# Attention feeding a gated feed-forward layer: two state reads moved from chunk 0 to chunks 3 to 5, and one intermediate kept on chip

## The chip, the cores and the metric

The kernel runs on one core of one Trainium2 chip. A core has five engines with a queue of instructions each: PE (TensorE, the matmul array), DVE (VectorE), ACT (ScalarE), POOL (GpSimd) and SP (SyncE, which here only starts transfers). The metric is the time of one execution on the device in microseconds (us); a run of the same kernel differs from another by about 0.3%.

## The reference

A batch has 8 heads, 512 tokens and 32 state rows of 64 numbers. Tokens attend to the state rows ("xread"), state rows attend to the tokens ("sread"); both go, as 4608 rows of 512, through a feed-forward layer with 2048 hidden units. `x` is scaled up by 3.377, the two weights are given in 64 bits.

```python
B, H, S, Ns, D = 8, 8, 512, 32, 64          # d_model = H * D = 512, d_ff = 2048
scores  = scale * matmul(x, state.T)        # (B, H, S, Ns)
a       = exp(scores - max);  a  /= a.sum(-1) + 1e-9
xread   = matmul(a, state)
scores2 = scale * matmul(state, x.T)        # the same numbers, transposed
a2      = exp(scores2 - max); a2 /= a2.sum(-1) + 1e-9
sread   = matmul(a2, x)
x = concatenate([xread, sread], axis=2).transpose(0, 2, 1, 3).reshape(B * (S + Ns), H * D)
h = x @ w_in
return (h - tanh(h)) @ w_out
```

## The kernel before

**Chunks and steps.** The 512 tokens of batch i are chunk i (0 to 7); the 256 state rows of all batches are chunk 8. A chunk has 16 steps, one for each 128 hidden units, and step `st = 16*i + f` of the outer loop writes the hidden units two steps ahead (`LAG = 2`, `hidden`), whatever is planned for that step, and then the output matmuls of its own step (`output`). So batch 0's last part is written in steps 0 to 15, batch 4's in steps 64 to 79.

**The feed-forward layer.** xread is never formed. Since `(a @ state) @ w_in = a @ (state @ w_in)`, `hidden` multiplies the attention weights `aT` with `m = state @ w_in` of that batch into the bank `hps` (L375, L376, L377: each 32-bit factor is split into a rounded part and a rest, and three of the four products are kept). `finish` takes tanh on ACT and subtracts on DVE (both L383: tile `t`), then `split` makes `g`: the rounded part on ACT (L90), the rest on DVE (L91). `add` accumulates into `ops` from `g` and the converted `wo`: rounded `g` by rounded `wo` (L413), rounded `g` by the rest of `wo` (L414), the rest of `g` by rounded `wo` (L415). The rest of `wo` comes from DVE, its rounded part from ACT.

**Chunk 0 carries the conversions.** The weights come in as 64-bit numbers and are made into 32-bit ones, block by block (16 blocks `wo0` to `wo15` of `w_out`, 16 blocks `wqp` of `w_in`): DVE L120, DVE L121, ACT L123, DVE L124. A block of `w_out` is then split into `wo` (ACT L90, DVE L91). A block of `w_in` goes to DRAM (`wf`) and is at once multiplied by the states of batches 0 and 1 (`m_first_two`, L149). Batch 0's half of the result is copied by ACT to `m_first` (L150). Batch 1's half is copied to a tile `stage` (L152), written to DRAM (L153, for the first four blocks L587 and L590), and read back in chunk 0 and 1 as `mr` (L200). The same products for batches 2 to 7 are made later by `m_units` (`wst`, L186, L187, L188, L191), with two buffers of `stage`.

**Attention of a batch** (`attention`): scores by matmul into `sps`, copied to `s` (L273), then the softmax over states on a transposed copy `e`, transposed back to `at` and split into `aT`. Batches 0 and 1 (`b < LONE`) use block-diagonal states and 64 columns of the array (L254, and L517 for batch 0), the others 32 columns in eight tiles (L262). **The state read** (`state_read`) starts from the same scores `s`: for each half of the heads DVE takes a maximum (L306) and makes small factors (L308, L312, L313), ACT the exponential in place (L310), SP loads the tokens `xn` (L316, 512 KB), PE turns the weights (`pps`, L319), ACT copies them (`p2t`, L321), PE multiplies (`rps`, L329: 64 columns for `b < LONE`, else 32), and DVE scales the result into `sr` (L335, four instructions). `sr` is read in chunk 8 only. In batch 0 the state read also splits `at` into `aT0`, with the rest made on POOL.

**What sets the order.** The start is written out by hand (`SEQ`). After it, a table (`SCH`) says in which step each part of `conv`, `wo`, `pair` (the calls of `m_first_two`), `a0` (batch 0's state read, four parts), `att` (the attention of batches 1 to 7, with their state reads) and `m0`, `m1` (the units) is written; a scheduler then orders each engine's instructions from that, and `tc.issue_after(x)` holds an instruction behind `x`. All transfers stand in SP's queue in one order.

Of the kernel before, what the change touches and what calls it, by code (L numbers as in the profile page):

```python
# [9 lines left out]
F32 = mybir.dt.float32  # L10
# [9 lines left out]
P = 128  # L20
B, H, S, NS, D = 8, 8, 512, 32, 64
# [6 lines left out]
LAG = 2  # L28
LONE = 2


@with_exitstack
def attention_ffn(ctx: ExitStack, tc: tile.TileContext, xT, xn, bd, bh, sp, sm, sl, win, wout, xout, sout):
# [106 lines left out]
    XSUB = nc.gpsimd if '1' else None  # L140

    def m_first_two(q, p):
# [6 lines left out]
        nc.tensor.matmul(ps, sps[:, p], wfs[q, k][:, c], start=True, stop=True)  # L149
        nc.scalar.copy(m_first[q][64 * c : 64 * c + 64, k], ps[0:64])  # L150
        stage = pool.tile([P, 2, 512], F32, tag="stage", name=f"st0{q}{p}", bufs=SB)
        nc.scalar.copy(stage[64:128, 0], ps[64:128])  # L152
        nc.sync.dma_start(  # L153
            mdram[1][q][0][k, 2 * c : 2 * c + 2].rearrange("h n f -> (h n) f"), stage[64:128, 0]
        )

# [37 lines left out]
    def load_m(b, q):  # L194
        if b == 0:
            r = m_first[q]
# [36 lines left out]
    def attention(b, aT):  # L233
# [51 lines left out]
        for hf in range(2):  # L285
# [224 lines left out]
    def step(op):  # L510
# [7 lines left out]
        elif k == "c":  # L518
            ss[j] = pool.tile([P, 512], F32, tag="s", name=f"s0{j}")
            o(nc.scalar.copy(ss[j], sps_ps[j]))  # L520
# [60 lines left out]
        elif k == "R":  # L581

            if j % 2 == 0:
                stages[j // 2] = pool.tile([P, 4, 256], F32, tag="stage", name=f"st00{j}", bufs=SB)
            st = stages[j // 2]
            with tc.issue_after(tanhs[RE[j]][0]):
                nc.scalar.copy(st[64:128, :, P * (j % 2) : P * (j % 2) + P], mps[j][64:128])  # L587
            if j % 2:
                for k in range(2):
                    nc.sync.dma_start(  # L590
                        mdram[1][0][0][k, :, :, P * (j - 1) : P * (j + 1)].rearrange("(c h) n f -> (h n) c f", c=2),
                        st[64:128, 2 * k : 2 * k + 2],
                    )

# [50 lines left out]
    for i in range(B + 1):  # L645
        for f in range(NFF):
# [24 lines left out]
            for b in range(1, B):  # L671
                n = D0["att"][str(b)].count(st)
                if n:
                    if b not in atts:
                        atts[b] = new_attention(b)
                    advance(atts[b], n)
            for g in range(2):
                advance(m1[g], D0[f"m{g}"].count(st))
            chunks[i].output(f)
# [49 lines left out]
```

## Time and profile before

| | |
|---|---|
| median of 3 runs | 688.42 us (687.70 to 689.92) |
| the profiled execution | 688.88 us, of which the profile's span is 687.1 us |
| granted TensorE clock, mean over the span | 0.988 |
| busy share of the span | PE 96%, DVE 67%, ACT 55%, POOL 1% |
| moved by DMA | 99.30 MB, 145 GB/s on average |

Chunk 0's output matmuls end near 142 us. In the profile an instruction's row gives its start, its duration, its engine, its line in the kernel and the tiles that it writes and reads. Of matmuls in a row the starts are the measure: they overlap by about 0.17 us. A number in brackets behind a row is the time that the engine was idle before it, and what it waited for. "PEld" loads the weights of a matmul beside PE. The clock column gives the share of full speed that the PE's clock was granted.

### The profile page before, as it was taken

What the parts mean: (1) busy time and instruction counts of PE and PEld (TensorE: products, weight loads), DVE (VectorE), ACT (ScalarE), POOL (GpSimd) and SP (SyncE); (2) the same over time, 40 slices, a digit from 0 to 9 for tenths busy, and PEclk for the clock granted to TensorE, in tenths of its full rate; (3) what the DMA queues carried; (4) which work ended last, traced back from release to release, by engine and by line L of the source; (5) the groups of instructions that cost most, each with busy time, mean ns of one, the idle gap of its engine ahead of it and who ended that gap; (6) DMA issues with size and microseconds to landing.
All of it is one profiled execution on the core that took longest, in us unless ns stands there. A gap on an engine that the chain in (4) does not pass through costs nothing.

```text
span 687.1 us, 9286 instructions
## 1 busy us (share of the span) xinstructions
PE 660.5 (96%) x3386; PEld 521.7 (76%) x3386; DVE 458.2 (67%) x803; ACT 377.9 (55%) x663; POOL 6.6 (1%) x11
## 2 busy tenths in 40 slices
PE   4788988999999999999999999999999999999997
PEld 2446666888788887888788878887878788888896
DVE  5897999965695559556876568546853587434442
ACT  3768876766675655457656555634433354333342
POOL 2100000000000000000000000000000000000000
PEclk9899998999999999999999999999999999999999
DMA  8888972555545552345536432643241312001310
GB/s 292 252 300 257 340 275 93 183 185 144 169 122 188 150 168 97 124 126 162 175 124 203 133 106 86 220 145 127 89 157 44 124 48 95 28 14 41 131 32 31
DMA packets 46317, 99.30 MB, mean 145 GB/s; under 512 B 6208, under 2 KB 12096, under 8 KB 46272
## 3 DMA queue, kind: packets, MB, share of 16 engines
q1 hardware_dynamic: 46272, 98.72, 44.4%
q8 instruction: 26, 0.43, 0.3%
q14 instruction: 19, 0.16, 0.1%
HBM read 66.72 MB, written 31.98 MB: 144 GB/s over the span
## 4 chain that ended last, share of the span: by engine, by line
PE 85%; DMA 6%; DVE 4%; ACT 3%; issue 1%; SPq 0%; ACTq 0%; DVEq 0%
PE ops L413 17%; PE ops L414 17%; PE ops L415 17%; PE hps L376 9%; PE hps L377 9%; PE hps L375 9%; PE mps L187 2%; PE sps L262 1%; PE rps L329 1%; DMA mr<-md 1%; PE mps L186 1%; DMA w01d<-in_win 1%; DMA wf<-w 1%; PE pps L319 1%; DMA w31d<-in_win 1%; DMA wo1d<-in_wout 1%
## 5 line engine op out<-in xcount | busy, mean ns | idle before, releaser
L414 PE MATMUL ops<-wo,g 128*128 128x512 f32 x544 | 215.5, 396 | 2.1 <-DVE wo L91 2.1
L413 PE MATMUL ops<-wo,g 128*128 128x512 f32 x544 | 208.1, 397 | 3.1 <-ACT wo L90 3.1
L415 PE MATMUL ops<-wo,g 128*128 128x512 f32 x544 | 208.4, 394 | 0.0
L383 DVE TENSOR_TENSOR t<-hps,t 128x512 f32<-128x512 f32 (+1 forms) x142 | 93.3, 658 | 98.4 <-ACT t L383 97.5
L383 ACT ACTIVATE t<-hps 128x512 f32<-128x512 f32 (+1 forms) x142 | 81.1, 573 | 133.7 <-PE hps L377 131.4
L413 PEld LDWEIGHTS ops<-wo,g 128*128 128x128 f32 x544 | 102.4, 189 | 32.1 <-ACT wo L90 5.8
L90 ACT CAST g<-t 128x512 fp32r<-128x512 f32 (+1 forms) x142 | 84.6, 596 | 72.9 <-DVE t L383 56.6
L414 PEld LDWEIGHTS ops<-wo,g 128*128 128x128 f32 x544 | 103.2, 190 | 26.5 <-DVE wo L91 3.3
L91 DVE TENSOR_TENSOR g<-t,g 128x512 fp32r<-128x512 f32 (+1 forms) x142 | 93.3, 657 | 42.4 <-ACT g L90 41.1
L415 PEld LDWEIGHTS ops<-wo,g 128*128 128x128 f32 x544 | 102.8, 189 | 24.5 <-issue 2.4
L375 PE MATMUL hps<-aT,m 128*128 128x512 f32 x248 | 98.3, 397 | 0.0
L377 PE MATMUL hps<-aT,m 128*128 128x512 f32 x248 | 97.1, 393 | 0.6 <-DVE m L91 0.6
L376 PE MATMUL hps<-aT,m 128*128 128x512 f32 x248 | 97.0, 391 | 0.0
L377 PEld LDWEIGHTS hps<-aT,m 128*128 128x128 f32 x248 | 46.7, 188 | 11.0 <-DVE m L91 1.0
L91 DVE TENSOR_TENSOR wst<-w,wst 64x512 fp32r<-64x512 f32 x64 | 43.9, 686 | 16.4 <-ACT wst L90 15.0
L375 PEld LDWEIGHTS hps<-aT,m 128*128 128x128 f32 x248 | 46.6, 188 | 10.5 <-issue 0.7
L376 PEld LDWEIGHTS hps<-aT,m 128*128 128x128 f32 x248 | 46.7, 188 | 10.0 <-issue 0.5
L91 DVE TENSOR_TENSOR m<-mr,m 128x1024 fp32r<-128x1024 f32 x31 | 37.8, 1220 | 9.3 <-ACT m L90 8.6
L188 ACT COPY st<-mps 128x512 f32<-128x512 f32 x64 | 36.7, 587 | 12.3 <-PE mps L187 12.0
L90 ACT CAST wst<-w 64x512 fp32r<-64x512 f32 x64 | 39.6, 619 | 1.8 <-ACT wo13r L123 1.0
L90 ACT CAST m<-mr 128x1024 fp32r<-128x1024 f32 x31 | 32.3, 1043 | 7.3 <-DMA mr<-md 7.2
L187 PE MATMUL mps<-wst,sms 128*128 128x512 f32 x64 | 24.7, 394 | 0.0
(218 smaller groups left out, 587.6 us busy)
## 6 DMA issues: line engine op xcount, KB each, us to landing
md<-st SPq DMA_DIRECT2D x144, 128.0 KB, 2.2
mr<-md SPq DMA_DIRECT2D x28, 512.0 KB, 4.0
xT<-in_xT SPq DMA_DIRECT2D x16, 512.0 KB, 4.6
xn<-in_xn SPq DMA_DIRECT2D x16, 512.0 KB, 4.2
w<-wf SPq DMA_DIRECT2D x16, 512.0 KB, 4.6
out_x<-ob SPq DMA_DIRECT2D x32, 256.0 KB, 2.1
wn<-wf SPq DMA_DIRECT2D x8, 512.0 KB, 3.8
ml<-md SPq DMA_DIRECT2D x8, 512.0 KB, 3.6
```

The costliest lines, as they stand in the source:

```text
L90: nc.scalar.copy(hi, src)
L91: return (sub or nc.vector).tensor_sub(lo, src, hi)
L186: nc.tensor.matmul(ps, s[:, 1, h], t[:, e], start=True, stop=False)
L187: nc.tensor.matmul(ps, s[:, 0, h], t[:, e], start=(g == 1), stop=True)
L188: nc.scalar.copy(stage[:, e], ps)
L375: nc.tensor.matmul(ps, mhi[k][:, cols], ahi[:, k], start=(k == 0), stop=False)
L376: nc.tensor.matmul(ps, mhi[k][:, cols], alo[:, k], start=False, stop=False)
L377: nc.tensor.matmul(ps, mlo[k][:, cols], ahi[:, k], start=False, stop=(k == nk - 1))
L383: tanhs.append((nc.scalar.activation(t, ps, AF.Tanh).ins, nc.vector.tensor_sub(t, ps, t).ins))
L413: nc.tensor.matmul(o, g[:, 0, tok], wo[:, f, 0], start=(f == 0), stop=False)
L414: nc.tensor.matmul(o, g[:, 0, tok], wo[:, f, 1], start=False, stop=False)
L415: return nc.tensor.matmul(o, g[:, 1, tok], wo[:, f, 0], start=False, stop=(f == NFF - 1)).ins
```

## The change

- **State reads.** The state reads of batches 0 and 1 leave `attention`. Batch 0's four parts (`a0`) go from steps 0, 0, 1, 13 to 58, 60, 62, 64, batch 1's (`r1`, before at the end of its attention in steps 11 and 13) to 74, 76, 78, 80. Their scores `s` stay in four tiles of their own until then (`EARLY_S = 2`). The split of `aT0`, which stood in batch 0's state read, is written in the start, and its rest is made on DVE instead of POOL.
- **Batch 1's state @ w_in stays on chip.** `m_second[q]` takes the place of `stage` and DRAM: 16 writes of 128 KB and 4 reads of 512 KB go. For q = 0 and 1 it sits in the two `stage` buffers. The four copies of the first four blocks (L587) become eight of half the size.
- **Columns.** `LONE = 1`: batch 1's scores use the eight tiles of 32 columns, and the state reads of batches 0 and 1 the 32-column form.
- **Order.** In steps below 48 (`GATED`) what is planned for a step is held behind the tanh pair of that step, and the first four `m0` units go from steps 11, 11, 15, 15 to 16, 17, 18, 19.

```diff
-LONE = 2
+GATED = 48
+EARLY_S = 2
+LONE = 1
...
+    def second(q):
+        if q < 2:
+            return pool.tile([P, 2, 512], F32, tag="stage", name=f"mr1{q}", bufs=SB)
+        return pool.tile([P, 2, 512], F32, tag=f"mr1{q}", name=f"mr1{q}", bufs=1)
...
+            m_second[q] = second(q)
         ps = bank(ps_a, f"mps0{q}{p}")
         nc.tensor.matmul(ps, sps[:, p], wfs[q, k][:, c], start=True, stop=True)
         nc.scalar.copy(m_first[q][64 * c : 64 * c + 64, k], ps[0:64])
-        stage = pool.tile([P, 2, 512], F32, tag="stage", name=f"st0{q}{p}", bufs=SB)
-        nc.scalar.copy(stage[64:128, 0], ps[64:128])
-        nc.sync.dma_start(
-            mdram[1][q][0][k, 2 * c : 2 * c + 2].rearrange("h n f -> (h n) f"), stage[64:128, 0]
-        )
+        nc.scalar.copy(m_second[q][64 * c : 64 * c + 64, k], ps[64:128])
...
-        yield from state_read(b, ss)
+        if b >= EARLY_S:
+            yield from state_read(b, ss)
+        else:
+            late[b] = ss
...
+    def late_read(b):
+        yield from state_read(b, late[b])
+
+    def split_first():
+        for hf in range(2):
+            split(aTs[0][:, 0, hf], aTs[0][:, 1, hf], ats[hf])
...
-                split(aTs[0][:, 0, hf], aTs[0][:, 1, hf], ats[hf], nc.gpsimd if P0[4] else None)
...
-            w = 2 if b < LONE else 1
+            w = 1
...
     a0 = state_read(0, ss)
+    split_first()
+    late1 = late_read(1)
...
-    SCH = ... "a0": [0, 0, 1, 13], ... "m0": [11, 11, 15, 15, 20, ...
+    SCH = ... "a0": [58, 60, 62, 64], ... "m0": [16, 17, 18, 19, 20, ... "r1": [74, 76, 78, 80]
...
-            with tc.issue_after(first):
+            with ExitStack() as gates:
+                if st < GATED:
+                    for x in tanhs[st]:
+                        gates.enter_context(tc.issue_after(x))
                 advance(a0, D0["a0"].count(st))
+                advance(late1, D0["r1"].count(st))
                 ... attention and units, now inside the same block
```

The lines of the changed file stand a little lower: L90, L91 become L94, L95; L120, L121, L124 become L124, L125, L128; L149 becomes L161; L310, L319, L329 become L327, L336, L346; L383 becomes L400; L413, L414, L415 become L430, L431, L432.

**PE, early in chunk 0** (`pps00` and `rps00` are the first half of batch 0's state read, `pps01` begins the second; `mps013` is the product of `w_in` block 13 with the two states; `ops0_0` is the output bank of chunk 0, tokens 0 to 127). Before:

```order
L319 MATMUL pps00_369<-ident_72,s00_150 128x128 x4
L329 MATMUL rps00_376<-xn00_367,p2t00_374 64x128 x8
L149 MATMUL mps013_432<-w011_321,sps_126 128x512
L413 MATMUL ops0_0_389<-wo_77,g0_2_345 128x512
L413 MATMUL ops0_1_390<-wo_77,g0_2_345 128x512
L413 MATMUL ops0_2_391<-wo_77,g0_2_345 128x512
L413 MATMUL ops0_3_392<-wo_77,g0_2_345 128x512
L319 MATMUL pps01_449<-ident_72,s01_161 128x128 x4
L149 MATMUL mps020_562<-w020_468,sps_126 128x512
```

After:

```order
L161 MATMUL mps012_340<-w011_313,sps_118 128x512
L161 MATMUL mps013_387<-w011_313,sps_118 128x512
L430 MATMUL ops0_0_344<-wo_77,g0_2_337 128x512
L430 MATMUL ops0_1_345<-wo_77,g0_2_337 128x512
L430 MATMUL ops0_2_346<-wo_77,g0_2_337 128x512
L430 MATMUL ops0_3_347<-wo_77,g0_2_337 128x512
L161 MATMUL mps020_498<-w020_403,sps_118 128x512
```

The two parts of the state read no longer stand between the products `mps012`, `mps013`, `mps020` and the output matmuls of step 2. The first half's read now stands at row 1253 of PE's 2780, near the end of chunk 3.

**SP, the same time** (`xn` are the tokens of a state read, `md100` batch 1's product in DRAM, `wo1d` the raw second block of `w_out`). Before:

```order
L316 DMA xn00_367<-in_xn 128x1024
L552 DMA wf0_120<-w000_164 512x1x128
L316 DMA xn01_447<-in_xn 128x1024
L109 DMA w11d_198<-in_win 128x1024
L552 DMA wf0_120<-w000_164 512x1x128
L109 DMA w12d_236<-in_win 128x1024
L552 DMA wf0_120<-w002_217 512x1x128
L109 DMA w13d_256<-in_win 128x1024
L590 DMA md100_84<-st000_272 64x2x256 x2
L109 DMA wo1d_290<-in_wout 128x1024
L552 DMA wf0_120<-w002_217 512x1x128
```

After:

```order
L113 DMA w10d_174<-in_win 128x1024
L569 DMA wf0_112<-w000_156 512x1x128
L113 DMA w11d_190<-in_win 128x1024
L569 DMA wf0_112<-w000_156 512x1x128
L113 DMA w12d_228<-in_win 128x1024
L569 DMA wf0_112<-w002_209 512x1x128
L113 DMA w13d_248<-in_win 128x1024
L113 DMA wo1d_285<-in_wout 128x1024
```

The load of `wo1d` had two loads of `xn` and two writes of `md100` ahead of it, and has none of them now. Further down, the twelve writes of L153 leave their places between the loads of the weights, and both loads of `xT1` stand ahead of `wo5d`, where one of them stood behind `wo10d`.

**DVE, at the end of the conversions** (`wor14` and `wor15` are the last blocks of `w_out`; `wo_77<-` is the rest of a block, for which L414 waits). Before:

```order
L121 SCALAR_TENSOR_TENSOR wor15_1092<-wo15d_863,wor15_1092 128x512
L91 TENSOR_TENSOR wst003_1239<-w1001_1219,wst003_1239 64x512 x2
L91 TENSOR_TENSOR wo_77<-wor14_970,wo_77 128x512
L335 TENSOR_SCALAR sr0_78<-rps01_1138,ri01_444 32x64 x4
L91 TENSOR_TENSOR g1_0_1191<-t1_0_1188,g1_0_1191 128x512
L124 ISA wor15_1092<-wor15_1092,wo15r_1093 128x1024
L335 TENSOR_SCALAR sr0_78<-rps11_1151,ri11_1025 32x64 x4
L383 TENSOR_TENSOR t1_2_1288<-hps1_2_1281,t1_2_1288 128x512
L91 TENSOR_TENSOR wo_77<-wor15_1092,wo_77 128x512
```

After:

```order
L125 SCALAR_TENSOR_TENSOR wor14_864<-wo14d_778,wor14_864 128x512
L125 SCALAR_TENSOR_TENSOR wor15_925<-wo15d_788,wor15_925 128x512
L95 TENSOR_TENSOR g0_15_968<-t0_15_965,g0_15_968 128x512
L128 ISA wor14_864<-wor14_864,wo14r_865 128x1024
L128 ISA wor15_925<-wor15_925,wo15r_926 128x1024
L95 TENSOR_TENSOR g1_0_996<-t1_0_993,g1_0_996 128x512
L400 TENSOR_TENSOR t1_2_1055<-hps1_2_1048,t1_2_1055 128x512
L95 TENSOR_TENSOR wst002_1163<-w1001_1161,wst002_1163 64x512 x2
L95 TENSOR_TENSOR wo_77<-wor14_864,wo_77 128x512
L95 TENSOR_TENSOR m12_1344<-mr12_497,m12_1344 128x1024
L95 TENSOR_TENSOR wo_77<-wor15_925,wo_77 128x512
```

The eight scalings `sr` are gone from between the last two rests of `wo`; the rest of `wor14` and of `wor15` stand closer together, and the split of `m12` stands between them.

More of the change, by code (lines that the diff above doesn't have):

```diff
@@ L72, in attention_ffn @@
         [[dram.tile([2, 4, NS, 512], F32, name=f"md{b}{q}{i}") for i in range(1 if b < 6 else 2)] for q in range(NQ)]
+        if b >= 2
+        else None
         for b in range(B)
@@ L140, in attention_ffn @@
     XSUB = nc.gpsimd if '1' else None
+    m_second = {}
+    def second(q):
+        if q < 2:
+            return pool.tile([P, 2, 512], F32, tag="stage", name=f"mr1{q}", bufs=SB)
+        return pool.tile([P, 2, 512], F32, tag=f"mr1{q}", name=f"mr1{q}", bufs=1)
     def m_first_two(q, p):
@@ L194, in load_m @@
     def load_m(b, q):
-        if b == 0:
-            r = m_first[q]
+        if b < 2:
+            r = (m_first, m_second)[b][q]
         else:
@@ L271, in attention @@
             ps = pss[hf]
-            s = pool.tile([P, 512], F32, tag="s", name=f"s{b}{hf}")
+            s = pool.tile([P, 512], F32, tag=f"s{b}{hf}" if b < EARLY_S else "s", name=f"s{b}{hf}", bufs=1 if b < EARLY_S else 2)
             nc.scalar.copy(s, ps)
@@ L295, in attention @@
             yield split(aT[:, 0, hf], aT[:, 1, hf], at)
-        yield from state_read(b, ss)
+        if b >= EARLY_S:
+            yield from state_read(b, ss)
+        else:
+            late[b] = ss
+    late = {}
+    def late_read(b):
[3 more added lines that the diff above has]
+            split(aTs[0][:, 0, hf], aTs[0][:, 1, hf], ats[hf])
     def state_read(b, ss):
-        if b == 0:
-            for hf in range(2):
-                split(aTs[0][:, 0, hf], aTs[0][:, 1, hf], ats[hf], nc.gpsimd if P0[4] else None)
         for hf in range(2):
@@ L498, in attention_ffn @@
     m_first[0] = pool.tile([P, 2, 512], F32, tag="mr", name="mr00", bufs=RRB)
-    wb, stages, mps, sps_ps, hps, ss = {}, {}, {}, {}, {}, {}
+    wb, mps, sps_ps, hps, ss = {}, {}, {}, {}, {}
     es, ms, zs = {}, {}, {}
@@ L518, in step @@
         elif k == "c":
-            ss[j] = pool.tile([P, 512], F32, tag="s", name=f"s0{j}")
+            ss[j] = pool.tile([P, 512], F32, tag=f"s0{j}", name=f"s0{j}", bufs=1)
             o(nc.scalar.copy(ss[j], sps_ps[j]))
@@ L581, in step @@
         elif k == "R":
-            if j % 2 == 0:
-                stages[j // 2] = pool.tile([P, 4, 256], F32, tag="stage", name=f"st00{j}", bufs=SB)
-            st = stages[j // 2]
+            if j == 0:
+                m_second[0] = second(0)
             with tc.issue_after(tanhs[RE[j]][0]):
[L587 to L593, printed above, removed]
+                for c in range(2):
+                    nc.scalar.copy(m_second[0][64 * c : 64 * c + 64, :, j * P : j * P + P], mps[j][64:128, c::2])
     MP = [{"a": ps_a, "o": ps_o}[x] for x in 'oaoa']
@@ L617, in attention_ffn @@
     atts = {}
-    SCH = dict(json.loads('{"conv": [0, 1, 2, 2, 3, 3, 4, 4, 6, 7], "pair": [0, 1, 3, 3, 3, 3, 4, 5, 6, 7], "a0": [0, 0, 1, 13], "att0": [3, 5, 7, 7, 7, 8, 9, 11, 13], "att1": [6, 7, 8, 8, 11, 11, 11, 11, 13], "att2": [5, 9, 9, 13, 13, 13, 13, 13, 13], "m0": [11, 11, 15, 15, 20, 21, 21, 22, 22, 23, 25, 27, 29, 33, 35, 36], "m1": [40, 46, 52, 53, 53, 54, 55, 57, 62, 62, 62, 65, 73, 77, 79, 84], "wo": [0, 1, 2, 3, 4, 5, 6, 7, 8, 8, 9, 9, 10, 10, 12]}'))
+    SCH = dict(json.loads('{"conv": [0, 1, 2, 2, 3, 3, 4, 4, 6, 7], "pair": [0, 1, 3, 3, 3, 3, 4, 5, 6, 7], "a0": [58, 60, 62, 64], "att0": [3, 5, 7, 7, 7, 8, 9, 11, 13], "att1": [6, 7, 8, 8, 11, 11, 11, 11, 13], "att2": [5, 9, 9, 13, 13, 13, 13, 13, 13], "m0": [16, 17, 18, 19, 20, 21, 21, 22, 22, 23, 25, 27, 29, 33, 35, 36], "m1": [40, 46, 52, 53, 53, 54, 55, 57, 62, 62, 62, 65, 73, 77, 79, 84], "wo": [0, 1, 2, 3, 4, 5, 6, 7, 8, 8, 9, 9, 10, 10, 12], "r1": [74, 76, 78, 80]}'))
     D0 = dict(
@@ L668, in attention_ffn @@
                 m_first_two(*next(pairs))
-            with tc.issue_after(first):
+            with ExitStack() as gates:
+                if st < GATED:
+                    for x in tanhs[st]:
+                        gates.enter_context(tc.issue_after(x))
                 advance(a0, D0["a0"].count(st))
[L671 to L678, printed above, removed]
+                advance(late1, D0["r1"].count(st))
+                for b in range(1, B):
+                    n = D0["att"][str(b)].count(st)
+                    if n:
+                        if b not in atts:
+                            atts[b] = new_attention(b)
+                        advance(atts[b], n)
+                for g in range(2):
+                    advance(m1[g], D0[f"m{g}"].count(st))
             chunks[i].output(f)
```

2 lines of the change are left out of this document (1 added, 1 removed).

## The prediction

> **What bounds the kernel.** I read the busy line of the page first, then busy time by stretches, then what PE, DVE and SP wait for, and last single rows where two engines meet.
>
> ```profile
> PE 660.5 (96%) x3386; PEld 521.7 (76%) x3386; DVE 458.2 (67%) x803; ACT 377.9 (55%) x663; POOL 6.6 (1%) x11
> ```
> ```profile
> 0.00:33.00 33.00, 20.66 (x71) 11.19 (x71) 22.84 (x41) 17.65 (x32) 6.60 (x11) 0.90 0.84 271
> 33.00:70.00 37.00, 31.71 (x121) 20.12 (x121) 31.44 (x62) 27.81 (x50) 0.00 (x0) 0.95 0.87 284
> 70.00:143.00 73.00, 67.70 (x310) 50.81 (x309) 70.98 (x131) 53.54 (x93) 0.00 (x0) 0.95 0.61 209
> 145.00:683.00 538.00, 538.00 (x2881) 437.95 (x2879) 331.67 (x569) 277.05 (x486) 0.00 (x0) 1.00 0.37 118
> ```
>
> The columns of the stretches are its bounds and length, then PE, PEld, DVE, ACT and POOL busy (and their instructions), the granted clock, the share of the DMA engines, GB/s. From 145 us on PE has no gap at all and its full clock: there only matmul work counts. All that can be won by a better order lies before. There three regimes follow each other: to 70 us the DMA engines are busy 84 to 87% of the time and no compute engine is full; from 70 to 143 us DVE is full (70.98 of 73).
>
> ```profile
> PE ops L413 <- ACT wo L90: 3.1, 3, 1.7
> PE rps L329 <- ACT p2t L321: 2.2, 1, 2.2
> PE ops L414 <- DVE wo L91: 2.1, 3, 1.3
> PE mps L149 <- ACT st L152: 2.0, 1, 2.0
> ```
> ```profile
> DVE wor L120 <- DMA wo1d<-in_wout: 2.2, 1, 2.2
> DVE wor L120 <- DMA wo4d<-in_wout: 1.1, 1, 1.1
> DVE w L120 <- DMA w31d<-in_win: 1.1, 1, 1.1
> DVE w L120 <- PE mps L149: 1.0, 1, 1.0
> DVE w L124 <- ACT w20r L123: 0.9, 1, 0.9
> DVE z L289 <- ACT e L282: 0.8, 1, 0.8
> DVE wor L120 <- DMA wo5d<-in_wout: 0.6, 1, 0.6
> DVE w L120 <- DMA wf<-w: 0.3, 1, 0.3
> ```
> ```profile
> SPq L153 <- ACT st L152: 13.3, 10, 3.3
> ```
>
> These are the waits of PE (33 to 120 us), of DVE (20 to 112 us) and of SP (30 to 120 us): total, times, longest. PE waits in the end for converted blocks of `w_out`, whose rounded part is made behind DVE's conversion and whose rest DVE itself makes. DVE in turn is late because of the loads, and those are late in part because SP stands 13.3 us at writes of batch 1's product, with loads of weights queued behind. So the kernel's length is the time at which DVE has the late blocks ready, plus PE's work that is left then.
>
> ```profile
> 112.19 0.80 PE L414 MATMUL ops<-wo,g 128*128 128x512 f32 x1 [1.27 <-DVE wo L91]
> ...
> 135.05 0.39 PE L414 MATMUL ops<-wo,g 128*128 128x512 f32 x1
> ```
> ```profile
> 111.45 0.68 DVE L91 TENSOR_TENSOR wo<-wor,wo 128x512 fp32r<-128x512 f32 x1
> ...
> 132.58 0.69 DVE L91 TENSOR_TENSOR wo<-wor,wo 128x512 fp32r<-128x512 f32 x1
> 133.19 1.15 DVE L335 TENSOR_SCALAR sr<-rps,ri 32x64 f32<-32x64 f32 x4
> ```
>
> The rest of `wo10` is written from 111.45 and PE, having waited 1.27 us, uses it at 112.19: the last wait. The rest of `wo14` ends at 133.27 and is used at 135.05, 1.78 us later. From that use PE has 687.1 - 135.05 = 552.05 us left.
>
> **The change, part by part.** *PE's work.* The narrow forms are cheaper by these rows (starts of the group and of the instruction behind it):
>
> ```profile
> 77.93 1.08 PE L254 MATMUL sps<-xT,bdr 128*64 128x512 f32 x4
> 78.94 0.50 PE L414 MATMUL ops<-wo,g 128*128 128x512 f32 x1
> ```
> ```profile
> 183.87 1.09 PE L262 MATMUL sps<-xT,bdr 64*32 64x512 f32 x16
> 184.89 0.50 PE L415 MATMUL ops<-wo,g 128*128 128x512 f32 x1
> ```
> ```profile
> 129.39 1.97 PE L329 MATMUL rps<-xn,p2t 128*64 128x128 f32 x32
> 131.29 0.50 PE L375 MATMUL hps<-aT,m 128*128 128x512 f32 x1
> ...
> 218.79 0.65 PE L329 MATMUL rps<-xn,p2t 128*32 128x64 f32 x32
> 219.38 0.50 PE L186 MATMUL mps<-wst,sms 128*128 128x512 f32 x1
> ```
>
> Batch 1's scores: two halves of 1.01 us in the old form, the whole batch in 1.02 in the new, so -1.0. A half of a state read: 1.90 / 2 = 0.95 before (32 rows are two halves), and 0.59 in the new form; four halves, -1.4; the first half took 1.03, so I write -1.6. In all PE loses 2.6 us of work.
>
> By place: ahead of the use of `wo14`, all four reads of batches 0 and 1 and their transposes go away (5.2 us), as do 1.0 for the scores; some other rows come forward, and by the two orders, priced with such starts, 5.0 us less stands ahead. Only 2.6 are really gone, so 2.4 us more are left behind it: 552.05 + 2.4 = 554.45.
>
> *DVE's work.* In the late stretch an instruction starts about 0.6 us after the one before (the row of 132.58 and the next), four scalings `sr` take 1.2. Ahead of the rest of `wo14` the new order has none of 4 maxima (4 x 0.57, nearest row 132.58 to 133.19), 12 small ones (0.07, an estimate from the sum), 8 `sr` (2.4) and 2 `wst` (0.7 each); it has in addition 2 rests of `aT0`, one L124, one `g`, one `t` (0.6 each). That is 6.9 - 3.0 = 3.9; counted over all rows it is 4.0. The two rests of `aT0` are the price of taking them off POOL, and here is what they give back:
>
> ```profile
> 18.86 1.31 POOL L91 TENSOR_TENSOR aT<-at,aT 128x512 fp32r<-128x512 f32 x1 [5.76 <-ACT aT L90]
> 20.79 1.52 POOL L91 TENSOR_TENSOR aT<-at,aT 128x512 fp32r<-128x512 f32 x1 [0.61 <-ACT aT L90]
> ```
> ```profile
> 18.63 0.42 DVE L120 TENSOR_SCALAR w<-w02d 128x512 uint32<-128x512 uint32 x1
> ...
> 19.59 0.87 DVE L120 TENSOR_SCALAR w<-w03d 128x512 uint32<-128x512 uint32 x1
> 20.50 0.69 DVE L121 SCALAR_TENSOR_TENSOR w<-w03d,w 128x512 uint32<-128x512 uint32 x1
> 21.11 1.75 DVE L121 SCALAR_TENSOR_TENSOR w<-w02d,w 128x512 uint32<-128x512 uint32 x1
> ```
>
> Beside POOL's two subtractions DVE's L120 takes 0.87 instead of 0.42 and its L121 1.75 instead of 0.69, 1.5 us together. [...]
>
> *Waits that should go* (called w, with their rows above). The contention, 1.5. `wo1d`, 2.2: two loads of 512 KB and two writes of 128 KB, 1.25 MB, no longer stand ahead of it; at 284 GB/s that is 4.4 us of transfer, so I take 2.0. `wo4d` and `w31d`, 1.1 each: L153's writes leave the queue, but the buffers that these loads fill still have to come free; 1.5 of 2.2. The waits on PE's L149 and on `w20r`, 1.9: PE stood behind `p2t` and `st`, both gone from there (2.2 and 2.0 of PE); 1.0. Against that, `xT1`'s second load, 512 KB or 1.8 us at that rate, now stands ahead of `wo5d`; it waited 0.6 already, I add 0.5. w = 1.5 + 2.0 + 1.5 + 1.0 - 0.5 = 5.5. Its ends: 0, if each wait merely shows up at another instruction because the DMA engines stay full; and 9.5, if all eight waits of DVE (8.0) and the contention go.
>
> *Moved state reads.* Four halves of eight DVE instructions, two ACT instructions, a load of 512 KB and two PE groups now stand in chunks 3 to 5. PE's part there is counted above. DVE's and ACT's lie beside PE's work:
>
> ```profile
> 300.00:430.00 130.00, 130.00 (x713) 103.93 (x712) 88.44 (x156) 77.29 (x135) 0.00 (x0) 1.00 0.44 137
> ```
>
> DVE has 41 us free there of 130, ACT 52, the DMA engines over half. I cost it at nothing. If that cover failed, PE would stall at a `rps` that waits for `p2t`, 2.2 us as in the row above; but between `pps` and `rps` of a half stand 20 matmuls or more in the new order (4.5 us at 0.227), where in chunk 0 there was nothing. The loads `xn` take places on SP and two token buffers, which the next batch's `xT` needs; its scores come a chunk later.
>
> *The product kept on chip.* ACT copies as much as before, except eight copies for four (no more than +1 us, in the start, where ACT has 17.65 of 33 busy). 2 MB written and 2 MB read less; SP's 13.3 us go. `m0` begins with step 16, so its copies no longer crowd steps 11 to 15. Since `mr10` and `mr11` hold the two `stage` buffers, the first unit's load waits for their splits; both stand ahead of it in the order of ACT, so I cost that at nothing, at most one landing of a load late.
>
> *The sum.* The rest of `wo14` is ready at 133.27 - 4.0 - 5.5 = 123.8; PE uses it at once and then has 554.45 left: 678.2. That is 8.9 less than the span of 687.1, so 680.0 for the profiled execution (688.88). The median of the runs shown is 688.42, 0.46 lower than it: 679.5. Since in the old trace PE came 1.78 later than the block, 1.78 of the gain is that slack. The other block, `wo10`, gives less: 4.1 less DVE work and 1.1 more PE work left, 112.13 - 4.1 - 5.5 + 574.9 + 1.1 = 678.5 with the same throttling as before, and 3.4 less without it (below), so the two stand about level.
>
> **The rivals.** *The waits only move.* For it: the DMA engines are 84 to 87% busy up to 70 us, so the stream of weights may set DVE's pace whatever stands between. Then w is 0 to 2 and the gain 3.4 to 5.4: 683 to 685. Against it: bytes leave that stretch, 1 MB of state reads and a good MB of writes of the 19.4 MB that 0 to 70 carries (271 x 33 + 284 x 37 KB).
>
> *All waits go.* w = 9.5 and `wo10` does not come to bound: gain 3.4 + 9.5 = 12.9, 675.5. For it speaks that each of the eight waits has one place, ahead of which something is taken away; against it, that DVE then asks for the loads sooner than the DMA engines have brought them so far.
>
> *The clock.* The PE's clock falls when it starves:
>
> ```profile
> 108.00:120.00 12.00, 9.50 (x28) 7.06 (x28) 11.91 (x22) 7.63 (x14) 0.00 (x0) 0.72 0.14 49
> ```
>
> 12 x 0.28 = 3.4 us lie there. PE still outruns DVE in the new order, so a new dip can come, one or two steps later, where the slack behind is less: up to 3.4 on top, 683. [...]
>
> *Slower: a moved state read stalls SP.* Its `xn` and the next batch's `xT` share two token buffers, which only an earlier `rps` frees; behind them on SP stands `mr` of a later quarter.
>
> ```profile
> mr<-md SPq DMA_DIRECT2D x28, 512.0 KB, 4.0
> ```
>
> The worst place in the new order is the second half of batch 0's read: its `rps` stands 97 PE rows behind its `pps` (22 us), SP's second load of `xT5` waits for it, and `mr50` behind that load is first used 183 PE rows (41 us) after it. With 4.0 us of landing SP may stand 37 us too long before PE waits; every microsecond beyond is one on the time, and from 46 the kernel is slower than before; each of the other halves can add its own, and with 5 beyond in each of the four and that first place at 46 the time would be 703. For it: the two buffers are fewer than the transfers that now share them. *No change* would need w near -3, a new wait of 3 on DVE and none removed, which no row supports.
>
> **How the numbers follow.** Main case with or without a small dip of the clock, 677 to 682: 0.58. The waits only move, or the dip costs its 3.4, 682 to 685.5: 0.20. All go, 674.5 to 677: 0.13 (0.05 of it under 675). No difference (within 0.3%, 2 us, what a measurement of this kernel can tell): 0.03. Slower: 0.06. Predicted 679.5. The range 675 to 684.8 leaves out 0.05 below and about 0.11 above. Faster 0.91, same 0.03, slower 0.06.
>
> **What would show it.** Right: PE's waits for `p2t` and `st` gone before 60 us; SP without waits at L153's place; DVE's wait for `wo1d` under 0.5; no slow L120 and L121 near 20 us; the last rest of `wo` (137.5 before) near 125; no PE gap behind 130 us; the narrow `rps` at 0.59 a half. Wrong: DVE's idle time before 70 us as large as before under other names, PE gaps at `rps` or `hps` in chunks 3 to 5, or a clock under 0.97 over the span.

## The result and the profile after

The changed kernel takes 683.42 us (683.03 to 684.67, six runs) against 688.50 us: the ratio is 0.9921, with a 95% interval of 0.9899 to 0.9943. That is 5.1 us faster, where 8.9 were forecast. The profiled execution took 683.43 us; its span is 681.6, 5.5 less than before.

The page of the changed kernel, busy line, and its stretches with the columns of before:

```profile
PE 657.8 (97%) x3458; PEld 518.4 (76%) x3458; DVE 457.4 (67%) x805; ACT 378.5 (56%) x667; POOL 3.8 (1%) x9
```
```profile
33.00:70.00 37.00, 32.10 (x109) 20.28 (x108) 31.08 (x57) 28.94 (x50) 0.00 (x0) 0.95 0.86 301
70.00:143.00 73.00, 68.56 (x295) 51.31 (x294) 67.18 (x112) 52.73 (x91) 0.00 (x0) 1.00 0.51 165
108.00:120.00 12.00, 11.28 (x47) 8.16 (x46) 11.75 (x20) 8.77 (x15) 0.00 (x0) 1.00 0.15 40
```

From 33 to 70 us DVE is no busier than it was (31.08, before 31.44), although its later work was to move up; from 70 to 143 it is busy 3.8 us less, and the dip of the clock near 111 us is gone (1.00, before 0.72). What DVE waits for (20 to 112 us), and what SP waits for (30 to 120 us, its first row):

```profile
DVE wor L124 <- DMA wo2d<-in_wout: 3.3, 1, 3.3
DVE w L124 <- DMA w31d<-in_win: 2.6, 1, 2.6
DVE wor L124 <- DMA wo1d<-in_wout: 1.0, 1, 1.0
DVE g L593 <- ACT g L592: 0.3, 1, 0.3
```
```profile
SPq L113 <- DVE wor L125: 19.3, 8, 6.8
```

All eight old waits of DVE but those for `wo1d` and `w31d` are gone. But its waits for loads and stores of the weights are 6.9 us now and were 5.3 (2.2 + 1.1 + 1.1 + 0.6 + 0.3): a new one of 3.3 for `wo2d` came, and the one for `w31d` grew. SP no longer stands at the writes of batch 1's product, but 19.3 us at L113 (8.4 of them before 80 us): a load of a weight block that has no free buffer until DVE's L125 has read an older block.

PE's longest waits from 33 to 120 us:

```profile
PE ops L431 <- DVE wo L95: 4.5, 4, 2.2
PE mps L161 <- ACT mr L163: 2.5, 1, 2.5
```

The wait for `p2t` is gone. The one for the copy of batch 1's half (L152, 2.0 before) is still there under its new line, 2.5 at L163: the copy goes to another tile, but PE's bank comes free no sooner.

The two places on which the sum rested, DVE's rest of `wo14` and PE's first use of it:

```profile
124.44 0.69 DVE L95 TENSOR_TENSOR wo<-wor,wo 128x512 fp32r<-128x512 f32 x1
```
```profile
125.43 0.39 PE L431 MATMUL ops<-wo,g 128*128 128x512 f32 x1
```

The block comes 8.1 us earlier (132.58 before; forecast 9.5) and PE uses it 9.6 earlier (135.05; forecast 11.2). From that use PE has 681.6 - 125.43 = 556.2 us left, 4.1 more than the 552.05 of before, where 2.4 were forecast. So both terms missed by about 1.7, in the same direction.

Where the second part goes is seen by a method that works in this kernel because PE has no gap: the same output matmul is looked up in both traces, and the difference of its starts is PE's *lead*. Step 8 of chunk 2 (the first of its four L413) and step 0 of chunk 6 (group 96), before:

```profile
253.05 0.39 PE L413 MATMUL ops<-wo,g 128*128 128x512 f32 x1
...
504.62 0.39 PE L413 MATMUL ops<-wo,g 128*128 128x512 f32 x1
```

and after:

```profile
242.08 0.39 PE L430 MATMUL ops<-wo,g 128*128 128x512 f32 x1
...
499.42 0.39 PE L430 MATMUL ops<-wo,g 128*128 128x512 f32 x1
```

The lead is 10.97 us in chunk 2 and 5.20 in chunk 6, and stays 5.2 until the end. So the start of the kernel gained 11 us, and chunks 3 to 5, where the moved state reads now stand, gave 5.8 of them back.

### The profile page after: what moved, and what is told of

The parts are those of the page before. It is cut to its first block, busy times and chain, and to the rows that moved or that the text cites. A ratio compares the mean times of both kernels' runs of the same rounds, so it can differ in the third digit from the quotient of the medians.

```text
span 681.6 us, 9389 instructions
## 1 busy us (share of the span) xinstructions
PE 657.8 (97%) x3458; PEld 518.4 (76%) x3458; DVE 457.4 (67%) x805; ACT 378.5 (56%) x667; POOL 3.8 (1%) x9
## 4 chain that ended last, share of the span: by engine, by line
PE 81%; DVE 11%; DMA 4%; ACT 1%; issue 1%; SPq 0%; ACTq 0%; DVEq 0%
PE ops L430 16%; PE ops L432 16%; PE ops L431 16%; PE hps L392 8%; PE hps L393 8%; PE hps L394 8%; PE mps L195 2%; DVE t L400 1%; PE rps L346 1%; PE sps L270 1%; DVE wor L125 1%; PE pps L336 1%; DVE g L95 1%; DMA w01d<-in_win 1%; DMA wo2d<-in_wout 1%
## 5 line engine op out<-in xcount | busy, mean ns | idle before, releaser
L431 PE MATMUL ops<-wo,g 128*128 128x512 f32 x544 | 213.7, 393 | 4.5 <-DVE wo L95 4.5
L430 PE MATMUL ops<-wo,g 128*128 128x512 f32 x544 | 207.0, 395 | 0.6 <-ACT wo L94 0.5
L432 PE MATMUL ops<-wo,g 128*128 128x512 f32 x544 | 205.6, 391 | 0.0
L400 DVE TENSOR_TENSOR t<-hps,t 128x512 f32<-128x512 f32 (+1 forms) x142 | 93.7, 661 | 95.8 <-ACT t L400 95.1
L400 ACT ACTIVATE t<-hps 128x512 f32<-128x512 f32 (+1 forms) x142 | 81.6, 575 | 133.8 <-PE hps L394 130.0
L94 ACT CAST g<-t 128x512 fp32r<-128x512 f32 (+1 forms) x142 | 84.8, 598 | 73.7 <-DVE t L400 54.4
L431 PEld LDWEIGHTS ops<-wo,g 128*128 128x128 f32 x544 | 102.2, 188 | 28.8 <-DVE wo L95 7.5
L95 DVE TENSOR_TENSOR g<-t,g 128x512 fp32r<-128x512 f32 (+1 forms) x142 | 93.6, 660 | 45.0 <-ACT g L94 43.5
L430 PEld LDWEIGHTS ops<-wo,g 128*128 128x128 f32 x544 | 102.5, 189 | 27.9 <-ACT wo L94 3.0
L432 PEld LDWEIGHTS ops<-wo,g 128*128 128x128 f32 x544 | 102.0, 188 | 23.4 <-issue 1.3
L394 PEld LDWEIGHTS hps<-aT,m 128*128 128x128 f32 x248 | 46.6, 188 | 11.2 <-DVE m L95 1.5
L95 DVE TENSOR_TENSOR wst<-w,wst 64x512 fp32r<-64x512 f32 x64 | 43.9, 686 | 13.9 <-ACT wst L94 12.1
L95 DVE TENSOR_TENSOR m<-mr,m 128x1024 fp32r<-128x1024 f32 x31 | 37.9, 1223 | 8.0 <-ACT m L94 7.8
L94 ACT CAST wst<-w 64x512 fp32r<-64x512 f32 x64 | 39.7, 620 | 0.8
L94 ACT CAST m<-mr 128x1024 fp32r<-128x1024 f32 x31 | 32.3, 1045 | 3.5 <-DMA mr<-md 2.8
```

The source lines that it names most:

```text
L94: nc.scalar.copy(hi, src)
L95: return (sub or nc.vector).tensor_sub(lo, src, hi)
L394: nc.tensor.matmul(ps, mlo[k][:, cols], ahi[:, k], start=False, stop=(k == nk - 1))
L400: tanhs.append((nc.scalar.activation(t, ps, AF.Tanh).ins, nc.vector.tensor_sub(t, ps, t).ins))
L430: nc.tensor.matmul(o, g[:, 0, tok], wo[:, f, 0], start=(f == 0), stop=False)
L431: nc.tensor.matmul(o, g[:, 0, tok], wo[:, f, 1], start=False, stop=False)
```

## The experiments

Lead and giveback are read from each kernel's trace like this (giveback: lead in chunk 2 less lead in chunk 6); times and ratios are against the kernel before on the same chip. A lead is that of one execution, and executions of one kernel differ by some 1 us; the giveback repeats to 0.3 among kernels with the same form.

| kernel | median us | ratio (95%) | lead in chunk 2 | giveback |
|---|---|---|---|---|
| changed | 683.42 | 0.9921 (0.9899 to 0.9943) | 10.97 | 5.77 |
| e1, state reads back in chunk 0 | 686.02 | 0.9963 (0.9948 to 0.9978) | 3.69 | 0.05 |
| e2, these state reads left out | 678.37 | 0.9857 (0.9842 to 0.9872) | 10.53 | 0.06 |
| e3, before with late reads only | 686.85 | 0.9979 (0.9966 to 0.9992) | 10.03 | 7.83 |
| e4, product through DRAM | 682.38 | 0.9922 (0.9901 to 0.9943) | 13.09 | 5.77 |
| e5, rests of aT0 on POOL | 684.21 | 0.9926 (0.9903 to 0.9950) | 9.97 | 5.78 |
| e6, 64-column forms | 684.52 | 0.9932 (0.9909 to 0.9954) | 10.44 | 7.51 |
| e7, no holding behind tanh | 683.93 | 0.9926 (0.9903 to 0.9949) | 10.88 | 6.08 |
| e8, old steps of the units | 682.96 | 0.9912 (0.9894 to 0.9930) | 10.49 | 5.77 |
| g2, a fourth `parts` buffer | 681.74 | 0.9890 (0.9869 to 0.9911) | 13.66 | 5.77 |
| h1, before with that buffer | 686.86 | 0.9977 (0.9961 to 0.9994) | 3.47 | 0.00 |
| g1, product through DRAM, that buffer | 682.05 | 0.9899 (0.9882 to 0.9916) | 12.54 | 5.76 |
| h4, the same with a fifth | 682.49 | 0.9907 (0.9888 to 0.9926) | 13.30 | 6.00 |

**e1: the state reads back in chunk 0.**

```diff
-EARLY_S = 2
+EARLY_S = 0
...
-"a0": [58, 60, 62, 64]
+"a0": [0, 0, 1, 13]
...
-    late1 = late_read(1)
+    late1 = iter(())
```

> The changed kernel with one part undone: the state reads of batches 0 and 1 stand in chunk 0 again (steps 0, 0, 1, 13 and at the end of batch 1's attention); their 32-column form, the product kept on chip, the gates and the unit steps stay. Theory A (the gain comes from taking the reads out of chunk 0, where they cost PE 10 us with the waits around them, and 5.8 us of it are given back in chunks 3 to 5): some 4 us slower than the changed kernel's 683.4, 686 to 689. Theory B (the gain comes from the product kept on chip, since SP no longer stands at its writes; the moved reads are given back in full, because PE is full where they went): no slower than the changed kernel, 681 to 683.5.

It takes 686.02, and the ratio 0.9963 lies outside the changed kernel's interval. The difference of the ratios is 0.0042, 2.9 us, a little less than A expected; B falls. The lead says how: 3.69 instead of 10.97 in chunk 2, and nothing is given back later. So moving the reads is a trade: 7.3 us won in chunk 0, 5.8 paid in chunks 3 to 5. By the leads that leaves 1.5, less than the 2.9 by the ratios; the profiled execution of this kernel (685.02) was 1.0 under its median. What PE waits for in this kernel between 33 and 130 us shows what it was won from (its first two rows):

```profile
PE rps L346 <- ACT p2t L338: 3.7, 1, 3.7
PE hps L392 <- ACT aT L94: 2.2, 1, 2.2
```

The old wait of `rps` for `p2t` is back, and longer than before the change.

**e2: the same reads left out.**

```diff
-    a0 = state_read(0, ss)
+    a0 = iter(())
     split_first()
-    late1 = late_read(1)
+    late1 = iter(())
+    nc.gpsimd.memset(sr[0], 0.0)
```

> The changed kernel without the state reads of batches 0 and 1 altogether (their rows of sread are set to zero; it leaves out this part of the computation). It measures what the four late halves cost. The forecast's price, 0.35 + 0.59 us of PE a half: 3.8 us, 679.6. Theory A (each of the eight moved groups also lengthens the matmul ahead of it and the one behind it, about 0.2 us a group): 5.8 us, 677.6. If they cost nothing on the path: 683.4.

678.37, between the two prices, and by the difference of the ratios 4.4 us under the changed kernel. The trace decides more sharply: nothing is given back in chunks 3 to 5 (10.53, then 10.47), and the start is not faster than with the reads at their late place. So the giveback of 5.8 is the four late halves and nothing else, and it costs what A said. Counted over the trace from step 8 of chunk 1 to step 8 of chunk 5, before against after, the moved groups themselves take 3.87 more (transposes 1.53, reads 2.34), as forecast from their rows; another 1.95 lies on the matmuls around them. The rows of one late read show how that comes about:

```profile
372.89 0.39 PE L430 MATMUL ops<-wo,g 128*128 128x512 f32 x1
373.12 0.39 PE L431 MATMUL ops<-wo,g 128*128 128x512 f32 x1
373.44 0.65 PE L346 MATMUL rps<-xn,p2t 128*32 128x64 f32 x32
374.02 0.50 PE L195 MATMUL mps<-wst,sms 128*128 128x512 f32 x1
374.36 0.40 PE L432 MATMUL ops<-wo,g 128*128 128x512 f32 x1
```

The matmul ahead of the read takes 0.32 (373.12 to 373.44) where others take 0.227, the one behind it 0.34. Over the stretch the rows next to the transposes and reads come to 0.9 us more than in the trace without the moved reads. A second piece, against that trace, is that the scores of batch 5 now stand in two places, one of their eight matmuls alone and the other seven together, and each takes the time of the whole:

```profile
387.16 1.04 PE L270 MATMUL sps<-xT,bdr 64*32 64x512 f32 x2
388.13 0.50 PE L392 MATMUL hps<-aT,m 128*128 128x512 f32 x1
...
393.82 1.08 PE L270 MATMUL sps<-xT,bdr 64*32 64x512 f32 x14
394.83 0.50 PE L430 MATMUL ops<-wo,g 128*128 128x512 f32 x1
```

0.97 and 1.01, against 1.02 where the group is whole (each of these matmuls has two records, so x2 is one and x14 are seven). The kernel before has such a divided group too, so against it this is no loss, but a chance left out. Of the 1.95 about 1 us is then left. 0.8 of it lies on the second to sixth matmul behind a group of transposes, reads or scores (1.2 us over all of them, before 0.4); the trace without the moved reads has 0.8 there as well, so the reads alone don't explain it, and its cause stays open.

**e3: the late reads alone, on the kernel before.**

```diff
+EARLY_S = 2
...
-"a0": [0, 0, 1, 13]
+"a0": [58, 60, 62, 64], "r1": [74, 76, 78, 80]
```

(With the functions `late_read` and `split_first`, the four tiles of the scores and the smaller scratch area of the transfers, as in the changed kernel.)

> The kernel before with one part done: the state reads of batches 0 and 1 at the late steps, in their old 64-column form, the first split of aT0 still with POOL; the product still goes through DRAM. Theory A: faster than the kernel before by most of the change's 5.1 us, 683.5 to 686. Theory B: no faster, 687.5 to 690.

686.85, 0.21% faster (the interval leaves out no change, narrowly), between the two theories. The lead in chunk 2 is 10.03, within the scatter of the changed kernel's 10.97, so this one part makes the start about as fast as all parts together. But the wide form gives 7.83 back.

**e6: the 64-column forms.**

```diff
-LONE = 1
+LONE = 2
-            w = 1
+            w = 2 if b < LONE else 1
```

> The changed kernel with one part undone: batch 1's scores and the state reads of batches 0 and 1 in the 64-column form again. By the rows of the kernel before a late half costs 0.95 instead of 0.59 of PE, so the time given back in chunks 3 to 5 grows from 5.8 to 7.2 us, and the scores add up to 1.0 in chunk 0: 685 to 686. If the columns don't matter: 683.4.

684.52; the time is within the changed kernel's interval, a little under what was expected. The giveback is 7.51 instead of 5.77, 1.74 more where the rows of before said 1.44. So in the traces the narrow form takes 1.7 us off the price of the late reads; by their times the two forms are not told apart.

**e4: the product through DRAM again.**

```diff
-        nc.scalar.copy(m_second[q][64 * c : 64 * c + 64, k], ps[64:128])
+        stage = pool.tile([P, 2, 512], F32, tag="stage", name=f"st0{q}{p}", bufs=SB)
+        nc.scalar.copy(stage[64:128, 0], ps[64:128])
+        nc.sync.dma_start(mdram[1][q][0][k, 2 * c : 2 * c + 2]..., stage[64:128, 0])
...
```

(Behind the dots stand the copies and writes of the first four blocks and the loads of `mr`, which are those of before again.)

> The changed kernel with one part undone: batch 1's product goes through DRAM again (16 writes of 128 KB, 4 reads of 512 KB, with the copies and tiles of before). Theory A: little is lost, since DVE waits for loads in either case (6.9 us in the changed kernel's trace, 5.3 before): 683.4 to 685.5. Theory B: most of the gain is lost, 687 to 689.

The ratio is the changed kernel's (0.9922). Keeping the product on chip, with 4 MB less traffic and no wait at the writes, brings nothing that can be measured; theory B falls. The stretch from 33 to 70 us and DVE's three longest waits for loads in this kernel:

```profile
33.00:70.00 37.00, 33.17 (x117) 20.83 (x115) 33.47 (x61) 30.07 (x52) 0.00 (x0) 1.00 0.95 332
```
```profile
DVE wor L122 <- DMA wo1d<-in_wout: 1.8, 1, 1.8
DVE wor L122 <- DMA wo2d<-in_wout: 1.5, 1, 1.5
DVE w L122 <- DMA w31d<-in_win: 1.4, 1, 1.4
```

The DMA engines carry 332 GB/s here and 301 in the changed kernel, so in the changed kernel they were not at their limit; and with more traffic DVE waits less for loads (4.7 us for these three blocks, 5.3 with two waits of 0.3) than without (6.9). What holds the loads must be something else.

**g2: one more buffer.**

```diff
-    PB = int('3')
+    PB = int('4')
```

> The changed kernel with one number more: four instead of three buffers of the kind `parts`, so that six raw blocks of the weights are on their way instead of five. Theory C (DVE and the loads turn in a loop: a load waits until DVE has freed the buffer of five blocks ago, DVE waits for the load, so what is taken off SP's queue shows up as another wait of the same loop): DVE's waits for loads fall from 6.9 us to under 4 and the kernel gets 2 to 3 us faster, 680.5 to 681.5. Theory D (the DMA engines, 86% busy from 33 to 70 us, set the pace): the waits stay near 7 us, 683 to 684.5.

681.74, ratio 0.9890. DVE's waits in the start, all of them:

```profile
DVE w L124 <- issue: 2.7, 2, 1.9
DVE wor L124 <- DMA wo2d<-in_wout: 2.2, 1, 2.2
DVE z L297 <- ACT e L290: 0.2, 1, 0.2
DVE wor L124 <- DMA wo3d<-in_wout: 0.2, 1, 0.2
```

Waits for loads fall from 6.9 to 2.4, under the 4 that theory C named. But the two waits under "issue" (2.7), for which the view names no cause, end with a transfer too. A converted block of `w_in` is written into one of two tiles, and by these rows a tile is written again only when its store to `wf` has landed:

```profile
41.91 0.42 SPq L480 DMA_DIRECT2D wf<-w  x1
```
```profile
50.27 0.43 DVE L124 TENSOR_SCALAR w<-w22d 128x512 uint32<-128x512 uint32 x1 [1.88 <-issue]
```

That store takes 8.3 us to land, until 50.18, and DVE starts at 50.27, though `w22d` itself landed at 40.7; the other wait, 0.8 us, ends at 32.88 behind a store that landed at 32.80. So all waits on transfers fall from 6.9 to 5.1 only, 1.8 less: part of the wait has moved once more, from loads to stores. The gain of 1.7 us by the medians is just under the 2 to 3 of theory C, and the intervals of the two ratios overlap; the lead grows by 2.7, but the profiled execution was 1.0 under the median of its runs. The time is under the range of theory D. So the loop of the buffers took what SP's emptier queue offered: a load waits for DVE to free the buffer of five blocks ago, DVE for the load.

**h1, g1, h4: the buffer elsewhere.** h1 is the kernel before, g1 and h4 are e4, with PB as 4, 4 and 5.

> The kernel before with only the fourth `parts` buffer (six raw blocks on their way instead of five; the room for it comes from a smaller scratch area of the transfers, which the kernel does not use). If the buffers are the loop that holds DVE in the start whatever else stands there: faster by about the 2 us that the same buffer gave to the changed kernel, 686 to 687. If before the change SP's 13 us at the writes of batch 1's product hold the loads, a sixth buffer can't be filled earlier: no gain, 688 to 689.

> The changed kernel with the product through DRAM again and the fourth `parts` buffer. If the buffers are the loop and the product's place does not matter, as the run with it in DRAM alone suggests: as fast as the changed kernel with four buffers, 681 to 682.5. If keeping the product on chip pays once the loop is loosened: slower by 1 to 3, 683 to 685.

> The same with a fifth `parts` buffer, for which the room of the product on chip is used. If the loop still binds at six blocks: 1 to 2 us faster than with four, 679.5 to 681. If the DMA engines set the pace by then: the same, 681 to 682.5.

h1 is 0.23% faster (1.6 us), and DVE's waits for loads fall from 5.0 us (5.3 with the store) to 2.9, although SP still stands 9.6 us at the writes of L153: a sixth block can be filled in spite of them. What the 1.6 us come from is open, though: DVE's rest of `wo14` starts at 132.47, as late as before (132.58), while the clock, 0.72 from 108 to 120 us before, has no dip in this execution:

```profile
108.00:120.00 12.00, 10.53 (x44) 7.92 (x44) 11.84 (x21) 9.63 (x17) 0.00 (x0) 1.00 0.12 44
```

g1 is as fast as g2 within its interval: with the loop loosened the product's place still does not show. h4 shows no gain over g1, so six blocks on their way are enough here; PE's lead of 14.7 us that this kernel has at the beginning of chunk 1 shrinks to 13.3 by chunk 2.

**e5: the rests of aT0 on POOL.**

```diff
-            split(aTs[0][:, 0, hf], aTs[0][:, 1, hf], ats[hf])
+            split(aTs[0][:, 0, hf], aTs[0][:, 1, hf], ats[hf], nc.gpsimd)
```

> The changed kernel with one part undone: the rests of aT0 are made on POOL again. The forecast's term (contention of 1.5 against 1.2 of own work on DVE): DVE's L124 and L125 near 20 us slow again, and the kernel 0.3 to 1.5 slower, 683.7 to 685. If the load waits that follow at 38 to 44 us take it up whole: 683.4.

684.21, not told apart from the changed kernel by time. The contention shows in the rows; POOL and DVE in this kernel:

```profile
18.58 1.31 POOL L95 TENSOR_TENSOR aT<-at,aT 128x512 fp32r<-128x512 f32 x1 [5.76 <-ACT aT L94]
21.43 1.27 POOL L95 TENSOR_TENSOR aT<-at,aT 128x512 fp32r<-128x512 f32 x1 [1.55 <-ACT aT L94]
```
```profile
18.68 0.70 DVE L557 STREAM_TRANSPOSE at<-e 128x512 f32<-128x512 f32 x1
19.30 0.87 DVE L124 TENSOR_SCALAR w<-w03d 128x512 uint32<-128x512 uint32 x1
20.21 0.69 DVE L125 SCALAR_TENSOR_TENSOR w<-w03d,w 128x512 uint32<-128x512 uint32 x1
...
21.64 1.61 DVE L128 CUSTOM_DVE_ANT_0 w<-w,w02r 128x1024 uint16<-128x1024 uint16 x1
```

and L124 and L128 in the changed kernel:

```profile
19.22 0.39 DVE L124 TENSOR_SCALAR w<-w03d 128x512 uint32<-128x512 uint32 x1
...
21.93 0.69 DVE L128 CUSTOM_DVE_ANT_0 w<-w,w02r 128x1024 uint16<-128x1024 uint16 x1
```

L124 starts at 19.30, POOL ends at 19.89, and L124 ends at 20.17; L128 starts at 21.64, POOL ends at 22.70, L128 at 23.25. Both begin while a subtraction of POOL runs, and each ends behind it by a little less than its own time in the changed kernel (0.28 of 0.39 and 0.55 of 0.69). L125, which starts at 20.21 between POOL's two, takes its usual 0.69. The transpose of 18.68 keeps its 0.70 with POOL beside it all the time, so not every DVE instruction is hit. In these two rows the contention cost a little less than what was left of POOL's instruction when DVE's began: 0.5 and 0.9 us, with 0.6 and 1.1 left. What the two engines contend for is not shown.

**e7 and e8: the order.** In e7 `GATED = 0`; in e8 `"m0"` begins with 11, 11, 15, 15.

> The changed kernel with one part undone: nothing is held behind the tanh pair of its step (GATED = 0). If the holding carries part of the gain (the attention of batch 1 and the units no longer go ahead of the conversions on DVE): PE's lead over the kernel before in chunk 1 falls from 11.0 to about 8, 685 to 687. If it only sets the order off the path: 683 to 684.

> The changed kernel with the first four units at their old steps 11, 11, 15, 15. They bring their copies, casts and rests back beside the last conversions, where DVE is full: the rests of wo14 and wo15 come 2 to 3 us later (four rests of 64 rows at 0.7), 684.5 to 686. If the holding behind the tanh pair keeps them back in any case: 683.4.

Neither is told apart from the changed kernel by time (0.9926 and 0.9912). In e7 the lead in chunk 1 does fall, as the first of its two expectations said: 7.1 us at step 0 and 8.7 at step 8, where the changed kernel has 11.0. But PE has done 18 matmuls more by step 0 (4.1 us at 0.227), and by step 8 of chunk 2, where both have done the same, the lead is 10.88. So the holding sets the order of the work and does not make the gain; in time the second expectation came true. In e8 the rests of `wo14` and `wo15` do come later, at 126.64 and 129.57 instead of 124.44 and 126.19, as expected, but the kernel is no slower: the lead is 8.7 at the beginning of chunk 1, with eight more matmuls done (1.8 us), and 10.49 in chunk 2. So the later blocks cost PE some 0.5 us, within the scatter of a lead, and not the 1 to 2 that were expected.

## Why the prediction was right, and where it was off

- **The direction and the place: right.** The time lies within the range, near its upper end, but not in the main case of 677 to 682: it falls into the bracket of "the waits only move". The start gained, PE has no gap behind 130 us but one of 0.3, and PE's wait for `p2t` is gone (its wait for the copy of the product, which was to go too, is not). Of the forecast's signs of being right, a wait for `wo1d` under 0.5 did not come (1.0), and the first sign of being wrong did: before 70 us DVE waits 7.2 us (3.3 + 2.6 + 1.0 + 0.3), and it waited 6.9 before, under other names. The forecast had the moved reads as "counted above" and their cover on DVE and ACT as enough: no gap at a late `rps` appeared, and the slower rival, SP standing behind a token buffer, did not come.
- **w, 5.5 forecast, about 4 measured.** The rest of `wo14` came 8.1 us earlier; with 4.0 less work that leaves 4.1. Term by term: the contention gave 1.9 instead of 1.5. The subtraction that closes this stretch on DVE starts 1.1 earlier (before, then after), though two rests of 0.6 were put ahead of it; 0.4 of this was there ahead of POOL's first subtraction, since L120 of `w02d` starts at 18.63 before and as L124 at 18.27 after:

```profile
23.61 0.68 DVE L569 TENSOR_TENSOR t<-hps,t 128x512 f32<-128x512 f32 x1
```
```profile
18.27 0.42 DVE L124 TENSOR_SCALAR w<-w02d 128x512 uint32<-128x512 uint32 x1
...
22.53 0.69 DVE L586 TENSOR_TENSOR t<-hps,t 128x512 f32<-128x512 f32 x1
```

  The waits behind PE and ACT gave 2.4 instead of 1.0 (1.0, 0.9 and 0.8 gone, 0.3 new). The step that failed is the one on the loads. It had `wo1d` come 2.0 earlier because transfers ahead of it on SP go away, and 1.5 for `wo4d` and `w31d`; instead all waits for loads and stores together grew by 1.6. (1.9 + 2.4 - 1.6 = 2.7; of the other 1.4, 0.4 is the earlier start named above, and the last 1.0 is not traced to rows.) So the loads fell 4.6 short of their 3.0, and that the other terms made up 3.2 of this is luck. `wo1d` did land 1.9 earlier, and `w31d` 2.7; but DVE was ready for them earlier too, by 0.8 and 4.1, and still waits for both. DVE at `w31d`, before and after:

```profile
60.99 0.43 DVE L120 TENSOR_SCALAR w<-w31d 128x512 uint32<-128x512 uint32 x1 [1.13 <-DMA w31d<-in_win]
```
```profile
58.33 0.43 DVE L124 TENSOR_SCALAR w<-w31d 128x512 uint32<-128x512 uint32 x1 [2.57 <-DMA w31d<-in_win]
```

  The rest of the 8.1 us arises behind this row: from it to the rest of `wo14` DVE is busy 3.4 us less (69.2, then 65.8) and idle 2.0 less (2.37, then 0.34). The forecast looked at what stands ahead of a load on SP and named, in passing, that "the buffers that these loads fill still have to come free"; SP's 19.3 us at L113 and g2 show that this binds, and the two tiles of converted blocks next to it. The rival "the waits only move" was right on these waits, and wrong on why: it put them down to busy DMA engines, and e4 carries 10% more.
- **PE's work left, +2.4 forecast, +4.1 measured.** The forms were priced right (0.35 and 0.59 a half, 3.87 in all for the late ones). Mis-sized is the term by what a group does to its neighbours, 0.9, and by the rest of the 1.95 around the groups, whose cause is open.
- **The product kept on chip: nothing.** The forecast gave it SP's 13.3 us as a cause of late loads; e4 and g1 show no gain from it. What it bought is room in SP's queue that brought no time.
- **The clock** did not dip in the start behind 70 us (1.00 from 70 to 143), as the main case allowed; ahead of that it was as before (0.90 to 33 us, 0.95 to 70). For "falls when it starves" the trace of before has its four stretches at 0.50 (20 to 22, 30 to 32, 54 to 56 and 112 to 118 us), each behind one in which PE had little or nothing to do (0.00 of 2 us busy from 15.5 to 17.5 and from 26 to 28, 0.00 of 1.8 from 51.1, 1.69 of 4 from 108). But from 45 to 47 PE did nothing either (0.00 of 2), and the clock stayed at 1.00 to 53: idle time goes ahead of each dip there, but does not bring one each time.

What carries the change: in time about half each, the late place of the reads and the other parts together. Of the 0.79%, 0.42 go when the reads stand in chunk 0 again (e1), and the 0.37% that are left come from the other parts, none of which alone is told apart by time. Alone and in the wide form the late reads make 0.21% (e3). In the traces they bring a lead of 10 us, and the narrow form brings the giveback from 7.5 or 7.8 to 5.8. The version with the fourth buffer (g2) is faster than the kernel before, and by medians and lead also than the changed one.

## What to carry to other kernels

Work moved out of a crowded start to a stretch where one engine is full is paid there in that engine's time, so the gain is the difference: price the moved groups with the matmuls next to them, and choose their cheapest form first. When a wait for a load goes away, ask what the load itself waits for: with a fixed set of buffers that the waiting engine frees, an emptier queue moves the wait to another block, and here one more buffer (1.7 us) was worth more than 4 MB less traffic (nothing measurable). Where one engine has no gaps, the difference of the starts of the same instruction in two traces tells to a few tenths of a microsecond where a change gives back; what the start gained scatters by about 1 us from one execution to the next.

## What the runs showed of the hardware

- A group of small matmuls cost its neighbours in the changed kernel: ahead of each of its 16 32-column reads the 512-column matmul takes 0.32 instead of 0.227 us (start to start), behind one 0.34, behind four transposes 0.31 (331.00 to 331.31 in the row below and the next).

```profile
330.64 0.60 PE L336 MATMUL pps<-ident,s 128*128 128x128 f32 x4
331.00 0.48 PE L430 MATMUL ops<-wo,g 128*128 128x512 f32 x1
331.31 0.40 PE L431 MATMUL ops<-wo,g 128*128 128x512 f32 x1
```

- A group of eight score tiles takes 1.02 whole; divided into one and seven it takes 0.97 and 1.01. In the trace the seven start within 0.05 us of each other (393.82 to 393.86), and the eighth alone takes as long as they do.
- 355 GB/s were moved from 33 to 70 us in h4, with the DMA engines 98% busy; 284 before and 301 after the change, with 87 and 86%, were not their limit.

```profile
33.00:70.00 37.00, 33.82 (x126) 22.34 (x128) 33.74 (x61) 32.17 (x55) 0.00 (x0) 1.00 0.98 355
```
